# Crossbar transposes for the attention output, and VectorE's part of a first-layer step emitted one step later

## Chip, core and metric

One Trainium2 chip, one of its cores. The metric is the device time of one execution in microseconds; a run of the kernel before and one of the kernel after are compared on the same chip. TensorE is PE, VectorE is DVE, ScalarE is ACT, GpSimd is POOL, SyncE is SP.

## What is computed

Chunked attention over four sequences of 768 positions (8 heads of 64), then a two-layer network on the 3072 resulting rows of 512 numbers:

```python
# per chunk c of 32 positions: keys and values from 16 before to 8 behind it, and 8 memory rows
scores = scale * np.matmul(q_c, k_full.transpose(0, 1, 3, 2))
a = softmax(scores)
out[:, :, c_start:c_end] = np.matmul(a, v_full)
...
x = np.ascontiguousarray(attn_out.transpose(0, 2, 1, 3)).reshape(B * S, H * D)   # 3072 x 512
h = x @ w_in                      # 512 x 2048
s = np.sin(alpha * h)
g = h + s * s / (alpha + 1e-09)
return (g @ w_out).astype(np.float32)   # 2048 x 512
```

## The kernel before

The four sequences (batches) go through one after the other, and the attention of batch i+1 is woven into the second layer of batch i. All matmul operands are bf16, and PE accumulates in PSUM. PSUM is divided into two pools: `big` has three tiles of two banks each (`sc`, `ot`, `hT`, and most of the transposed q and k, `tt_b`), `smp` two tiles of one bank each (`o`, `tt_a`, the split `hs`, `xtp`).

**Attention** (`burst`, L311). A batch has eight blocks of 96 positions. `qk_exp` (L262) computes a block's scores for the eight heads with eight matmuls into `sc` (L266), and ACT takes the exponential into `pt` in three pieces (L275). `pv` (L282) multiplies `pt` with the values, to which a column of ones is added (eight matmuls, L288), and DVE divides by the sum: a reciprocal (L292) and a product (L293) into `x_blk`, 96 positions on partitions by 512 numbers. The first layer needs this with the 512 numbers on partitions. `xt` (L300) makes that: four PE transposes (L306) of 96x128 into PSUM and one DVE copy (L309) into `xT`. For batches 1 to 3 these four go into a part of the bank of `ot` that `pv` has left free; for batch 0 into a tile of `smp`. The burst runs as a software pipeline: in step s the scores of block s, then `pv` of block s-lag, then `xt` of block s-lag-1. Between these three, `stream.take(n)` puts n matmuls of the previous batch's second layer into PE's queue; the numbers are written out by hand in `shares`.

**First layer** (`l1`, L333). A step ft computes 128 of the 2048 hidden columns for all 768 positions: four 128-row slices of the contraction times two halves of 384 positions, eight matmuls (L341) into `hT`, kt outermost. ACT takes the sine into `u` (L353). The square `s2` is taken by ACT, DVE or POOL, as a string of letters says (A, D, P; L356 and L358), and DVE computes gT = s2/alpha + h from PSUM (L367; in two halves, L363, for three steps of batch 0). Only then is the `hT` tile free. Sixteen steps make a batch. In batches 1 to 3, `stream.take(2)` or `take(3)` puts second-layer matmuls of the batch before ahead of each step. In batches 1 and 2 every second step also transposes two heads of the q or k of the batch after the next attention (`piece`): POOL or DVE pairs heads (L226), PE transposes (L242 for k, L257 for q) into the one tile of `smp` that `o` leaves, and DVE copies k (L243, L249) or ACT copies q (L258) to SBUF. Batch 0 does all its eight pieces after its first layer.

**Second layer** (`l2`, L371). Six subtiles of 128 rows per batch, sixteen matmuls of 128x512 each (L393) into `o`, then a copy to `o_sb` by DVE or ACT (L400, L402) and a store by SP (L403). `l2` is a generator; `Stream.take` (L30) advances it. Unless `through` is set, a take stops at the end of a subtile and keeps what is left as a debt for the next take.

**Order.** Each engine runs its instructions in the order in which the program emits them, and waits in place for what an instruction needs; there is no scheduler that moves them. SP's queue holds the output stores; POOL's queue issues the loads of q, k, v and the weights beside POOL's own work. The loads of batch 2 are issued between the pieces and the burst at the end of batch 0, those of batch 3 at the end of batch 1's first layer.

Of the kernel before, what the change touches and what calls it, by code (L numbers as in the profile page):

```python
# [9 lines left out]
P = 128  # L10
QW = 96
NEG = -30000.0
KW = 856
BF = mybir.dt.bfloat16
F32 = mybir.dt.float32
ACTF = mybir.ActivationFunctionType
ALU = mybir.AluOpType
# [28 lines left out]
def kernel(  # L46
# [12 lines left out]
    nc = tc.nc  # L59
    B, H, S, D = q.shape  # L60
# [3 lines left out]
    NJ = S // QW  # L64
    HP = H // 2
    FT = d_ff // P
    KT = d_model // P
    NSUB = S // P
    HALF = S // 2
# [3 lines left out]
    xp = ctx.enter_context(tc.tile_pool(name="xp", bufs=2))  # L73
    gp = ctx.enter_context(tc.tile_pool(name="gp", bufs=2))
    mlp = ctx.enter_context(tc.tile_pool(name="mlp", bufs=3))
    blk = ctx.enter_context(tc.tile_pool(name="blk", bufs=3))
    big = ctx.enter_context(tc.tile_pool(name="big", bufs=3, space=bass.MemoryType.PSUM))
    smp = ctx.enter_context(tc.tile_pool(name="smp", bufs=2, space=bass.MemoryType.PSUM))

# [15 lines left out]
    w_in_sb = consts.tile([P, KT, d_ff], BF, name="w_in_sb")  # L95
    w_out_sb = consts.tile([P, FT, d_model], BF, name="w_out_sb")
    alpha_sb = consts.tile([P, FT], F32, name="alpha_sb")
    inv_alpha = consts.tile([P, FT], F32, name="inv_alpha")
# [13 lines left out]
    def load_qk(b):  # L112
        kb, qb = alloc_qk()
        for src, dst in ((k, kb), (q, qb)):
            nc.gpsimd.dma_start(
                dst[:].rearrange("p h r d -> p h (r d)"),
                src[b].rearrange("h (p r) d -> p h (r d)", p=P),
            )
        return kb, qb
# [47 lines left out]
    def spin(n):  # L167

        z = smp.tile([P, 512], F32, name="z", tag="sm")
        for _ in range(n):  # L170
            nc.tensor.matmul(z[:], zeros[:, 0:P], zeros[:])  # L171
# [19 lines left out]
    for c0, c1, thr, val in (  # L191
# [4 lines left out]
            out=biasm[:, c0:c1], in_=biasm[:, c0:c1],  # L196
# [27 lines left out]
    def pair_up(src, hp, eng=None):  # L224
        pr = blk.tile([P, 6, 2, D], BF, name="pr")
        (eng or nc.gpsimd.tensor_copy)(  # L226
            pr[:].rearrange("p r e d -> p e r d"), src[:, 2 * hp:2 * hp + 2]
        )
        return pr
# [52 lines left out]
    def pv(b, j, pt):  # L282
        x_blk = blk.tile([QW, H, D], BF, name="x_blk")
        rinv = blk.tile([QW, H], F32, name="rinv")
        ot = big.tile([P, 2, 512], F32, name="ot", tag="big")
        otv = ot[:, :, 0:4 * (D + 1)].rearrange("p g (e c) -> p g e c", e=4)
        for h in range(H):
            nc.tensor.matmul(  # L288
                otv[:, h // 4, h % 4, :], pt[:, QW * h:QW * h + P], vws[b % 2][:, h, j, 0:D + 1]
            )  # L290
        rv = rinv[:].rearrange("p (g e) -> p g e", g=2)
        nc.vector.reciprocal(rv, otv[0:QW, :, :, D])  # L292
        nc.vector.tensor_tensor(  # L293
            out=x_blk[:].rearrange("p (g e) d -> p g e d", g=2), in0=otv[0:QW, :, :, 0:D],
            in1=rv.unsqueeze(3).to_broadcast([QW, 2, 4, D]),
            op=ALU.mult,
        )
        return x_blk, ot

    def xt(xT, j, x_blk, ot):  # L300
        if ot is None:
            xtp = smp.tile([P, KT, QW], BF, name="xtp", tag="sm")[:]
        else:
            xtp = ot[:].bitcast(BF)[:, 0, 640:640 + KT * QW].rearrange("p (k c) -> p k c", k=KT)
        for kt in range(KT):
            nc.tensor.transpose(  # L306
                xtp[:, kt, :], x_blk[:, 2 * kt:2 * kt + 2, :].rearrange("p e d -> p (e d)"), ident[0:QW, 0:QW]
            )
        nc.vector.tensor_copy(xT[:, :, QW * j:QW * j + QW], xtp)  # L309

    def burst(b, stream, shares, lag):  # L311

        xT = xp.tile([P, KT, S], BF, name="xT")
        ptl, xbl = {}, {}
        for s in range(NJ + lag + 1):
            n = shares[s] if s < len(shares) else 0
            if s < NJ:
                ptl[s] = qk_exp(s)
            if b == 0:
                spin(1)  # L320
            stream.take(n // 3, True)
            if 0 <= s - lag < NJ:
                xbl[s - lag] = pv(b, s - lag, ptl.pop(s - lag))
                if b == 0:
                    xbl[s - lag] = (xbl[s - lag][0], None)
            stream.take((n + 1) // 3, True)
            if 0 <= s - lag - 1 < NJ:
                xt(xT, s - lag - 1, *xbl.pop(s - lag - 1))
            stream.take((n + 2) // 3, True)
        return xT  # L330


    def l1(i, ft, xT, gT, sq, split=False):  # L333
        if split:
            hts = [smp.tile([P, 512], F32, name="hs", tag="sm") for _ in range(2)]
        else:
            hT = big.tile([P, 2, 512], F32, name="hT", tag="big")
            hts = [hT[:, 0], hT[:, 1]]
        for kt in range(KT):
            for hf in range(2):  # L340
                nc.tensor.matmul(  # L341
                    hts[hf][:, 0:HALF],
                    w_in_sb[:, kt, P * ft:P * ft + P],
                    xT[:, kt, HALF * hf:HALF * hf + HALF],
                    start=(kt == 0), stop=(kt == KT - 1),
                )
        u = mlp.tile([P, 2, HALF], F32, name="u")
        if split:
            for hf in range(2):
                nc.scalar.activation(  # L350
                    u[:, hf], hts[hf][:, 0:HALF], ACTF.Sin, scale=alpha_sb[:, ft:ft + 1])
        else:
            nc.scalar.activation(u[:], hT[:, :, 0:HALF], ACTF.Sin, scale=alpha_sb[:, ft:ft + 1])  # L353
        s2 = mlp.tile([P, 2, HALF], F32, name="s2")
        if sq == "A":
            nc.scalar.activation(s2[:], u[:], ACTF.Square)  # L356
        else:
            (nc.vector if sq == "D" else nc.gpsimd).tensor_tensor(  # L358
                out=s2[:], in0=u[:], in1=u[:], op=ALU.mult)
        gv = gT[:, ft, :].rearrange("p (e c) -> p e c", e=2)  # L360
        for hf in range(2):
            if split:
                nc.vector.scalar_tensor_tensor(  # L363
                    out=gv[:, hf], in0=s2[:, hf], scalar=inv_alpha[:, ft:ft + 1],
                    in1=hts[hf][:, 0:HALF], op0=ALU.mult, op1=ALU.add)
            elif hf == 0:
                nc.vector.scalar_tensor_tensor(  # L367
                    out=gv, in0=s2[:], scalar=inv_alpha[:, ft:ft + 1],
                    in1=hT[:, :, 0:HALF], op0=ALU.mult, op1=ALU.add)

    def l2(i, gT, last=False):  # L371
        for s in range(NSUB):
# [61 lines left out]

    stream = Stream()
    xT = burst(0, stream, (), 2)
    put_memk(1)
    put_memv(1)

    for i in range(B):  # L440
        gT = gp.tile([P, FT, S], BF, name="gT")
        last = i == B - 1
        at_ft = {2 * n: n for n in range(8)}
        pieces = []
        if not last:
            srcs = [(kq_next[n % 2], n // 2) for n in range(2 * HP)]
        state["pools"] = 1

        def pair_to(n):
            while len(pieces) < min(n, 2 * HP):  # L450
                pieces.append(pair_up(*srcs[len(pieces)], nc.vector.tensor_copy if i == 0 and len(pieces) % 2 == 0 else None))

        def piece(n):
            pair_to(n + 3)
            (t_k if n % 2 == 0 else t_q)(pieces[n], n // 2)

        if 0 < i < B - 1:
            pair_to(2)
        for ft in range(FT):
            sq = ("ADADADAAADADADAA" if i == 0 else "ADAAPDADADAPADAD")[ft]  # L460
            if 1 <= ft:
                stream.take(3 if last else 2)
            if 0 < i < B - 1 and ft in at_ft:
                piece(at_ft[ft])
            if i == 0 and ft == 14:
                pair_to(3)
            l1(i, ft, xT, gT, sq, i == 0 and ft in (3, 7, 11))
        stream.add(l2(i, gT, last))
        if not last:
            if i == 0:  # L470
                state["pools"], state["t"] = 3, 0
                stream.take(4)
                for n in range(2 * HP):
                    piece(n)
                    stream.take(3, True)
            if i + 2 < B:
                kq_next = load_qk(i + 2)
            if i == 0:
                xT = burst(i + 1, stream, (3, 3, 3, 4, 4, 4, 4, 4, 4, 4, 5, 5), 3)
            else:  # L480
                xT = burst(i + 1, stream, (16, 8, 6, 6, 6, 5, 5, 5, 5, 5), 1)
            if i + 2 < B:
                put_memk(i + 2)
            stream.take(3)
            if i + 2 < B:
                load_v_all(i + 2)
                put_memv(i + 2)
# [31 lines left out]
```

The softmax here doesn't subtract the row's maximum and nothing guards it: scores larger than these inputs give would overflow.

## Time and profile before

| What | us |
|---|---|
| Runs shown | 243.68, 243.36, 245.46 (median 243.68) |
| The profiled execution's own time | 245.14 |
| Its span, first to last instruction | 243.4 |
| PE busy | 222.6 (91%) |
| DVE busy | 160.2 (66%) |
| ACT busy | 154.7 (64%) |
| POOL busy | 73.3 (30%) |

The page of the profile gives the busy time of each engine, the chain of work that ended last, and the costliest groups of instructions. Some groups that the change touches:

| Group | Count | Busy us | Mean ns |
|---|---|---|---|
| L393 PE, second-layer matmul 128x512 | 368 recorded | 99.0 | 381 |
| L341 PE, first-layer matmul 128x384 | 488 recorded | 88.8 | 329 |
| L306 PE, transposes of x_blk into ot | 96 | 8.1 | 206 |
| L309 DVE, copy of ot to xT | 24 | 8.3 | 344 |
| L367 DVE, gT | 61 | 61.2 | 1012 |
| L358 DVE, square | 24 | 24.7 | 1029 |
| L293 DVE, x_blk | 32 | 22.0 | 686 |
| L243 DVE, copy of k | 16 | 13.6 | 852 and 854 |

A matmul's mean includes the time in which it overlaps its neighbours, since matmuls are pipelined; how closely they follow each other is read from their starts. The stages lie as follows: attention of batch 0 until 29.5 us, its first layer until 54, the pieces and the burst of batch 1 until 80.9, first layer of batch 1 until 112.6, burst of batch 2 until 134.5, first layer of batch 2 until 169.1, burst of batch 3 until 190.9, first layer of batch 3 until 222.5, the rest of its second layer until 243.4.

### The profile page before, as it was taken

To read this page: it belongs to the slowest core of one execution; us is meant where nothing else is said; L and a number is where in the kernel's file an instruction comes from. 1 tells how busy PE (TensorE), PEld (TensorE's weight loads), DVE (VectorE), ACT (ScalarE), POOL (GpSimd) and SP (SyncE) were. 2 spreads that over 40 slices of the span, in tenths; PEclk is the share of its full clock that TensorE was granted. 3 is DMA by queue.
4 is the path that set the end of the run, shared out by engine and by line. 5 is a ranking of instruction groups with operands and counts; after the bars stand their busy time and mean duration, and the time that the engine had idled before them with its cause. 6 is when DMAs were issued, how large, how long until landed. Compare 5 with 4: busy or idle time off the path is not lost.

```text
span 243.4 us, 4498 instructions
## 1 busy us (share of the span) xinstructions
PE 222.6 (91%) x1785; PEld 123.0 (51%) x1785; DVE 160.2 (66%) x287; ACT 154.7 (64%) x237; POOL 73.3 (30%) x96
## 2 busy tenths in 40 slices
PE   6798899989989899898999997998999999899994
PEld 2355565545445455454455653554455555453453
DVE  3496969999268658969457775868657267876101
ACT  3489599973975467798464784678765675871000
POOL 8899865214712114157200222120000002020000
PEclk9799999999999999999999997999999999999999
DMA  6999999999999610109992101001111101101122
GB/s 75 165 130 83 161 194 204 207 198 134 190 208 134 74 46 0 44 4 181 154 151 66 46 0 43 0 3 43 46 43 47 43 0 46 43 0 40 46 89 86
DMA packets 53852, 21.11 MB, mean 87 GB/s; under 512 B 36296, under 2 KB 50888, under 8 KB 53832
## 3 DMA queue, kind: packets, MB, share of 16 engines
q0 software_dynamic: 47616, 14.40, 70.7%
q1 hardware_dynamic: 6216, 6.43, 8.9%
q8 instruction: 14, 0.23, 0.4%
q14 instruction: 6, 0.05, 0.1%
HBM read 28.91 MB, written 6.29 MB: 145 GB/s over the span
## 4 chain that ended last, share of the span: by engine, by line
PE 48%; DVE 20%; ACT 12%; issue 12%; POOL 3%; DMA 2%; POOLq 1%; DVEq 0%; ACTq 0%
PE o L393 26%; PE hT L341 10%; DVE gT L367 8%; DVE s L358 5%; ACT pt L275 4%; ACT u L353 4%; ACT s L356 3%; PE ot L288 3%; PE sc L266 3%; POOL s L358 2%; DMA q_bf<-in_q_dram 2%; DVE kTi L243 2%; PE ot L306 2%; PE o L382 1%; DVE x_blk L293 1%
## 5 line engine op out<-in xcount | busy, mean ns | idle before, releaser
L393 PE MATMUL o<-w_out_sb,gT 128*128 128x512 bf16 x368 | 99.0, 381 | 0.7 <-DVE gT L367 0.4
L341 PE MATMUL hT<-xT,w_in_sb 128*128 128x384 bf16 x488 | 88.8, 329 | 3.9 <-DVE gT L367 3.6
L367 DVE SCALAR_TENSOR_TENSOR gT<-s,inv_alpha,hT 128x768 bf16<-128x768 f32 x61 | 61.2, 1012 | 30.0 <-ACT s L356 21.6
L353 ACT ACTIVATE u<-hT,alpha_sb 128x768 f32<-128x768 f32 x61 | 54.7, 898 | 28.3 <-PE hT L341 27.1
L341 PEld LDWEIGHTS <-w_in_sb 128*128 128x128 bf16 x512 | 49.8, 99 | 39.7 <-issue 7.4
L275 ACT ACTIVATE pt<-sc,biasm 128x256 bf16<-128x256 f32 x96 | 37.6, 492 | 13.0 <-PE sc L266 13.0
L393 PEld LDWEIGHTS <-gT 128*128 128x128 bf16 x368 | 31.9, 98 | 26.9 <-DVE gT L367 1.4
L358 POOL TENSOR_TENSOR s<-u 128x768 f32<-128x768 f32 x6 | 8.8, 1465 | 73.7 <-ACT u L353 73.7
L356 ACT ACTIVATE s<-u 128x768 f32<-128x768 f32 x34 | 28.7, 843 | 1.1
L358 DVE TENSOR_TENSOR s<-u 128x768 f32<-128x768 f32 x24 | 24.7, 1029 | 0.9 <-ACT u L353 0.8
L226 POOL COPY pr<-q_bf 128x768 bf16<-128x768 bf16 x12 | 10.1, 838 | 43.7 <-PE tt_a L242 27.4
L293 DVE TENSOR_TENSOR x_blk<-ot,rinv 96x512 bf16<-96x512 f32 x32 | 22.0, 686 | 1.1
L292 DVE RECIPROCAL rinv<-ot 96x8 f32<-96x8 f32 x32 | 6.4, 201 | 20.1 <-PE ot L288 19.8
L402 ACT COPY o_sb<-o 128x512 f32<-128x512 f32 x11 | 6.4, 585 | 20.0 <-PE o L393 20.0
L400 DVE COPY o_sb<-o 128x512 f32<-128x512 f32 x12 | 8.2, 687 | 15.4 <-PE o L393 15.4
L288 PEld LDWEIGHTS <-pt 128*128 128x128 bf16 x256 | 11.9, 97 | 7.2 <-issue 2.3
L171 PE MATMUL z<-zeros 128*128 128x512 bf16 x37 | 13.9, 463 | 1.3 <-DVE zeros L165 1.3
L288 PE MATMUL ot<-vw,pt 128*128 128x65 bf16 x256 | 13.0, 193 | 0.8 <-ACT pt L275 0.6
L266 PEld LDWEIGHTS <-kTi 64*128 64x128 bf16 x256 | 6.9, 94 | 13.0 <-issue 6.6
L266 PE MATMUL sc<-qT,kTi 64*128 64x96 bf16 x256 | 11.4, 205 | 1.8 <-ACT pt L275 1.2
L257 PEld LDWEIGHTS <-pr 128*128 128x128 bf16 x96 | 6.6, 100 | 12.5 <-issue 8.0
L306 PEld LDWEIGHTS <-x_blk 96*128 96x128 bf16 x128 | 8.4, 97 | 6.6 <-DVE x_blk L293 1.6
(66 smaller groups left out, 182.1 us busy)
## 6 DMA issues: line engine op xcount, KB each, us to landing
out_dram<-o_sb SPq DMA_DIRECT2D x23, 256.0 KB, 2.1
k_bf<-in_k_dram POOLq DMA_DIRECT2D x3, 768.0 KB, 8.6
q_bf<-in_q_dram POOLq DMA_DIRECT2D x3, 768.0 KB, 12.6
vw<-in_v_dram POOLq DMA_DIRECT2D x6, 384.0 KB, 17.4
w_in_sb<-in_moe_w_in_dram POOLq DMA_DIRECT2D x8, 256.0 KB, 8.3
w_out_sb<-in_moe_w_out_dram POOLq DMA_DIRECT2D x4, 512.0 KB, 18.7
k_bf<-in_k_dram POOLq DMA_DIRECT2D x4, 192.0 KB, 6.2
q_bf<-in_q_dram POOLq DMA_DIRECT2D x4, 192.0 KB, 6.7
```

The source lines that it names most:

```text
L171: nc.tensor.matmul(z[:], zeros[:, 0:P], zeros[:])
L266: nc.tensor.matmul(sc[:, e, QW * hp:QW * hp + QW], kTi[64 * e:64 * e + 64, hp, 104 * j:104 * j + P], qT[64 * e:64 * e + 64, hp, QW * j:QW ...
L275: nc.scalar.activation(pt[:, 0:H * QW].rearrange("p (g e c) -> p e g c", g=4, e=2)[:, :, :, 32 * m:32 * m + 32], sc[:, :, 0:4 * QW].rearra ...
L288: nc.tensor.matmul(otv[:, h // 4, h % 4, :], pt[:, QW * h:QW * h + P], vws[b % 2][:, h, j, 0:D + 1])
L293: nc.vector.tensor_tensor(out=x_blk[:].rearrange("p (g e) d -> p g e d", g=2), in0=otv[0:QW, :, :, 0:D], in1=rv.unsqueeze(3).to_broadcast( ...
L306: nc.tensor.transpose(xtp[:, kt, :], x_blk[:, 2 * kt:2 * kt + 2, :].rearrange("p e d -> p (e d)"), ident[0:QW, 0:QW])
L341: nc.tensor.matmul(hts[hf][:, 0:HALF], w_in_sb[:, kt, P * ft:P * ft + P], xT[:, kt, HALF * hf:HALF * hf + HALF], start=(kt == 0), stop=(kt ...
L353: nc.scalar.activation(u[:], hT[:, :, 0:HALF], ACTF.Sin, scale=alpha_sb[:, ft:ft + 1])
L356: nc.scalar.activation(s2[:], u[:], ACTF.Square)
L358: (nc.vector if sq == "D" else nc.gpsimd).tensor_tensor(out=s2[:], in0=u[:], in1=u[:], op=ALU.mult)
L367: nc.vector.scalar_tensor_tensor(out=gv, in0=s2[:], scalar=inv_alpha[:, ft:ft + 1], in1=hT[:, :, 0:HALF], op0=ALU.mult, op1=ALU.add)
L393: nc.tensor.matmul(o[:], gT[:, ft, P * s:P * s + P], w_out_sb[:, ft, :], start=(ft == 0), stop=(ft == FT - 1),)
```

## The change

In batches 1 to 3 the four PE transposes and the DVE copy of a block are replaced by one transposing DMA through the crossbar, from `x_blk` in SBUF to `xT` in SBUF, issued on SP's queue directly after `pv` of the same block. Batch 0 keeps the PE transposes. The pool of `x_blk`, `rinv` and `pr` has four buffers instead of three.

DVE's part of a first-layer step (the square where DVE takes it, and gT) becomes an inner function `finish`, which is called one step later: behind the second-layer matmuls and the piece that are emitted ahead of step ft+1, and before the matmuls of step ft+1. PE's, ACT's and POOL's parts stay in place.

The first step (ft = 0) of a batch runs the four slices of the first half of the positions, then those of the second half.

The hand-written shares of second-layer matmuls in the bursts are lower towards the end, and `stream.take` after a burst takes 8 (batch 0) or 12 instead of 3.

```diff
-    blk = ctx.enter_context(tc.tile_pool(name="blk", bufs=3))
+    blk = ctx.enter_context(tc.tile_pool(name="blk", bufs=4))
...
     def xt(xT, j, x_blk, ot):
-        if ot is None:
-            xtp = smp.tile([P, KT, QW], BF, name="xtp", tag="sm")[:]
-        else:
-            xtp = ot[:].bitcast(BF)[:, 0, 640:640 + KT * QW].rearrange("p (k c) -> p k c", k=KT)
+        if ot is not None:
+            nc.sync.dma_start_transpose(
+                xT[:, :, QW * j:QW * j + QW], x_blk[:].rearrange("p h d -> p (h d)"))
+            return
+        xtp = smp.tile([P, KT, QW], BF, name="xtp", tag="sm")[:]
...
             if 0 <= s - lag < NJ:
-                xbl[s - lag] = pv(b, s - lag, ptl.pop(s - lag))
-                if b == 0:
-                    xbl[s - lag] = (xbl[s - lag][0], None)
+                x_blk, ot = pv(b, s - lag, ptl.pop(s - lag))
+                if b > 0:
+                    xt(xT, s - lag, x_blk, ot)
+                else:
+                    xbl[s - lag] = x_blk
             stream.take((n + 1) // 3, True)
-            if 0 <= s - lag - 1 < NJ:
-                xt(xT, s - lag - 1, *xbl.pop(s - lag - 1))
+            if s - lag - 1 in xbl:
+                xt(xT, s - lag - 1, xbl.pop(s - lag - 1), None)
...
+        order = [(kt, hf) for kt in range(KT) for hf in range(2)]
+        if ft == 0:
+            order.sort(key=lambda o: o[1])
...
+        def finish():
+            if sq == "D":
+                nc.vector.tensor_tensor(out=s2[:], in0=u[:], in1=u[:], op=ALU.mult)
+            gv = gT[:, ft, :].rearrange("p (e c) -> p e c", e=2)
...
+        return finish
...
+        finish = None
         for ft in range(FT):
...
-            l1(i, ft, xT, gT, sq, i == 0 and ft in (3, 7, 11))
+            if finish is not None:
+                finish()
+            finish = l1(i, ft, xT, gT, sq, i == 0 and ft in (3, 7, 11))
+        finish()
...
-                xT = burst(i + 1, stream, (3, 3, 3, 4, 4, 4, 4, 4, 4, 4, 5, 5), 3)
+                xT = burst(i + 1, stream, (3, 3, 3, 4, 4, 4, 4, 4, 4, 4, 5), 3)
             else:
-                xT = burst(i + 1, stream, (16, 8, 6, 6, 6, 5, 5, 5, 5, 5), 1)
+                xT = burst(i + 1, stream, (16, 8, 5, 5, 5, 5, 5, 5, 3), 1)
...
-            stream.take(3)
+            stream.take(8 if i == 0 else 12)
```

More of the change, by code (lines that the diff above doesn't have):

```diff
@@ L338, in l1 @@
             hts = [hT[:, 0], hT[:, 1]]
[L339 to L346, printed above, removed]
+        order = [(kt, hf) for kt in range(KT) for hf in range(2)]
+        if ft == 0:
+            order.sort(key=lambda o: o[1])
+        for kt, hf in order:
+            nc.tensor.matmul(
+                hts[hf][:, 0:HALF],
+                w_in_sb[:, kt, P * ft:P * ft + P],
+                xT[:, kt, HALF * hf:HALF * hf + HALF],
+                start=(kt == 0), stop=(kt == KT - 1),
+            )
         u = mlp.tile([P, 2, HALF], F32, name="u")
@@ L356, in l1 @@
             nc.scalar.activation(s2[:], u[:], ACTF.Square)
[L357 to L369, printed above, removed]
+        elif sq == "P":
+            nc.gpsimd.tensor_tensor(out=s2[:], in0=u[:], in1=u[:], op=ALU.mult)
+        def finish():
+            if sq == "D":
+                nc.vector.tensor_tensor(out=s2[:], in0=u[:], in1=u[:], op=ALU.mult)
+            gv = gT[:, ft, :].rearrange("p (e c) -> p e c", e=2)
+            for hf in range(2):
+                if split:
+                    nc.vector.scalar_tensor_tensor(
+                        out=gv[:, hf], in0=s2[:, hf], scalar=inv_alpha[:, ft:ft + 1],
+                        in1=hts[hf][:, 0:HALF], op0=ALU.mult, op1=ALU.add)
+                elif hf == 0:
+                    nc.vector.scalar_tensor_tensor(
+                        out=gv, in0=s2[:], scalar=inv_alpha[:, ft:ft + 1],
+                        in1=hT[:, :, 0:HALF], op0=ALU.mult, op1=ALU.add)
+        return finish
     def l2(i, gT, last=False):
```

## The prediction

> **What bounds the kernel now.** I read first the table by stretches, with the cuts put where the batches' stages change, then the waits of TensorE, then the groups by form, then the timeline at the end of an attention burst, and last the DMA view of two stretches. Columns of the first fence: stretch, length, then busy time (and instructions) of PE, PE weight load, DVE, ACT and POOL, granted clock, DMA share, GB/s.
>
> ```profile
> 29.50:54.00 24.50, 22.96 (x140) 13.27 (x140) 21.74 (x28) 21.90 (x29) 10.11 (x11) 1.00 1.32 201
> 80.90:112.60 31.70, 27.82 (x190) 16.49 (x190) 24.10 (x34) 23.79 (x29) 12.10 (x12) 1.00 0.19 37
> 112.60:134.50 21.90, 21.90 (x237) 11.53 (x237) 14.19 (x31) 13.38 (x29) 3.39 (x5) 1.00 1.77 134
> 134.50:169.10 34.60, 31.30 (x205) 17.76 (x204) 24.70 (x33) 23.31 (x29) 7.12 (x7) 0.95 0.06 22
> 169.10:190.90 21.80, 21.76 (x231) 11.15 (x228) 13.51 (x29) 14.09 (x30) 0.00 (x0) 1.00 0.10 38
> ```
>
> The bursts of batches 2 and 3 (lines 3 and 5) are TensorE without a gap: work taken off PE there comes off the time. The first-layer stages of batches 1 and 2 (lines 2 and 4) leave PE idle for 3.9 and 3.3 us. Batch 0 (line 1) is bound by the DVE and ACT chain. Who stops PE:
>
> ```profile
> PE hT L341 <- DVE gT L367: 3.6, 6, 1.1
> ...
> PE tt_a L257 <- DVE o_sb L400: 3.1, 2, 1.7
> ...
> PE tt_a L257 <- DVE kTi L249: 2.4, 3, 1.0
> ```
>
> Total, times, longest. The last two are the transposes of q that wait for a PSUM tile which DVE has yet to empty; DVE is late because it stands in a previous step's gT. After the longest of them (1.73 us, until 147.72) the clock falls:
>
> ```profile
> 147.00:148.00 1.00, 0.28 (x5) 0.27 (x5) 1.00 (x3) 0.00 (x0) 0.00 (x0) 1.00 0.00 0
> 149.00:150.00 1.00, 1.00 (x5) 0.46 (x4) 0.66 (x1) 0.06 (x1) 0.22 (x1) 0.50 0.24 88
> ```
>
> The four stretches from 148 to 152 read 0.68, 0.50, 0.50 and 0.62: 0.32+0.50+0.50+0.38 = 1.7 us of PE work lost. A wait of 1.35 us (before 85.69) had no such drop.
>
> The end of the last burst, where the xT of the next first layer is completed:
>
> ```profile
> 187.57 0.41 PE L288 MATMUL ot<-vw,pt 128*128 128x65 bf16 x8
> 187.82 0.59 PE L393 MATMUL o<-w_out_sb,gT 128*128 128x512 bf16 x2
> 188.01 0.20 DVE L292 RECIPROCAL rinv<-ot 96x8 f32<-96x8 f32 x1 [0.31 <-PE ot L288]
> 188.25 0.33 PE L306 MATMUL ot<-ident,x_blk 96*128 96x96 bf16 x4
> 188.25 0.69 DVE L293 TENSOR_TENSOR x_blk<-ot,rinv 96x512 bf16<-96x512 f32 x1
> 188.42 1.24 PE L393 MATMUL o<-w_out_sb,gT 128*128 128x512 bf16 x5
> ...
> 190.75 1.46 PE L341 MATMUL hT<-xT,w_in_sb 128*128 128x384 bf16 x8
> ```
>
> From starts, since PE ends overlap: four transposes cost 188.42-188.25 = 0.17 us of PE; an L393 matmul 0.2155 us (five from 189.67, then 190.75); a first-layer step 1.30 us (8 x 0.163, from the chain of waits). The last x_blk is ready at 188.94, which is 1.12 us after PE is done with L288 (187.82).
>
> **The Trainium skill.** "VectorE: DVE Perf Modes", section "The three transpose paths", gives 1309 ns for a 128x128 bf16 crossbar transpose and 390 ns for TensorE's. No trace here has the first; the second is not borne out in this pipeline, where a 96x128 one costs PE 0.17/4 = 0.04 us. "Advanced Engine Details and Errata", section "X-Bar Transpose (TRN2)", says that transposing DMAs are as fast as ordinary ones; no run here shows it. "DMA: Bandwidth & Descriptors", section "Issuing engines are not separate DMA queues", says that DMAs of all queues interleave on the same 16 engines. The trace agrees: the same 256 KB output store lands in 2.0 us late in the kernel and in 5.5 us between 60 and 85 us, where the loads of batch 2 run:
>
> ```profile
> out_dram<-o_sb SPq DMA_DIRECT2D x13, 256.0 KB, 2.0
> ...
> out_dram<-o_sb SPq DMA_DIRECT2D x3, 256.0 KB, 5.5
> ```
>
> **The change, part by part.** *TensorE's transposes go* in batches 1 to 3: 3 x 8 x 0.17 = 4.1 us, all on the bound. The 24 DVE copies (L309, 0.344 us each, 8.3 us) go too; DVE has slack in the bursts (13.5 of 21.8 us), so they count nothing.
>
> *The deferral.* In every step DVE now meets the o_sb copy and the kTi copies of step ft+1 before the square and gT of step ft. ACT needs 0.90+0.84 us for sine and square before gT can run anyway, and the copies (0.85+0.31, or 0.69) mostly fit into that. The o_sb waits should go whole (3.1 us), of the kTi waits I count half (1.2), since the last steps of batch 1 are DVE-bound and only move the wait: 4.3 us, bounds 2 and 5.5. The clock drop went with the 1.73 us wait: 1.7 more. POOL's squares and ACT's part stay where they are. What can be late instead is hT: a gT behind both kTi copies comes up to 1.2 us later, and step ft+3 waits for that hT (three PSUM pairs). I count 0, since three steps take over 4 us of PE; bound +1.5.
>
> *The first step's order.* In batch 0 the first half no longer waits for the last xT copy; half of 1.30 us lies earlier: 0.6 us.
>
> *Gains:* 4.1+4.3+1.7+0.6 = 10.7 us.
>
> *What the crossbar adds.* On SP's queue, behind output stores, 24 DMAs of 96 KB; each waits for x_blk, so a store behind it waits too (o_sb has three buffers and a store comes every 4 us: free). x_blk has four buffers, so DVE stops if one takes longer than four blocks. And xT is now complete only when the last DMA lands. The PE order after the last L288 of a burst is 12, 9 and 9 second-layer matmuls (the take stops at a subtile's end), six key transposes (0.33 us) in batches 1 and 2, then the four first-half matmuls (0.65 us). Cover from x_blk to need, less the 1.12 us: batch 1 2.59+0.33+0.65-1.12 = 2.45; batch 2 1.94+0.33+0.65-1.12 = 1.80; batch 3 1.94+0.65-1.12 = 1.47 us. Issue to landing of one crossbar transpose isn't in the trace. From below: 1.7 us, the 128 KB store. From above: four times the skill's 1309 ns, 5.2 us. I take 3.0 us on free engines and 5.5 under load (the store's). Batch 1's burst lies wholly under the loads (they end at 81.5), batch 2's last blocks don't (129). Waits: 5.5-2.45 = 3.0; 3.0-1.80 = 1.2; 3.0-1.47 = 1.5; sum 5.7. The wait of 3.0 is longer than the one that dropped the clock: +1.7. The takes only move second-layer matmuls, 96 per batch as before: 0. More pr buffers: 0, no PE wait is on pr after batch 0.
>
> *Sum:* 10.7 gained, 7.4 given back: -3.3 us. The profiled execution took 245.14 us with a span of 243.4; it should become about 241.8 and 240.1. The median of the three runs shown is 243.68, 1.5 below the profiled one, so **240.4 us**.
>
> **Rivals.** *Crossbar hidden.* Landing in about 2.0 us, load or not: waits 0+0.2+0.5, no clock drop: -10, 233.7; with the deferral at its low bound and the +1.5, 237.5; I say 235.5. For it: 96 KB is less than a store. Against: stores go to 5.5 under load.
>
> *Slower: the crossbar queue falls behind.* Eight blocks must pass between the first x_blk and the need: in batch 1 66.99 to about 80.0 = 13 us, batch 2 118.5 to 133.8 = 15.3. That is 1.6 to 1.9 us per block. If a block occupies the queue longer than that, waits add up over eight. If each 1 KB row of x_blk went in four pieces (a guess), that is 384 packets, 24 per DMA engine; at the mean 56 ns of a packet on SP's queue (8.9% of 16 engines' 243.4 us over 6216 packets) 1.3 us, and beside loads, sharing the engines with them, twice that: 2.6. Then batch 1 waits 8x2.6+1-13 = 8.8, batch 2 about 5 (the loads end at 129), batch 3 1.5, and two clock drops 3.4: 18.7-10.7 = +8, 251.7; with part of the blocks after the loads, 249. It decides from about 2.1 us per block. For it: the DMA share of 1.8 to 2.5 in those bursts. At 5.2 us per block, eight take 42 us, some 28 more than there is, three times: above 300 us.
>
> *The deferral does nothing* because the waits move to hT: -10.7+6.0+7.4 = +2.7 at worst; with less waiting for xT 244.5.
>
> **How the numbers follow.** Within 1% is what a measurement of this kernel can't tell from no change: 241.2 to 246.1. Forecast 0.40 (238.5 to 243: 0.26 faster, 0.14 same), hidden 0.18 (faster), queue behind 0.30 (0.03 same, 0.27 slower), one block at 5.2 us 0.06 (slower), deferral idle 0.06 (0.05 same, 0.01 slower). Faster 0.44, same 0.22, slower 0.34. Range 235 to 252 leaves out the 5.2 us case, the upper part of the queue case and a little below. The forecast's own range is 238.5 to 243.
>
> **What would show it.** No L306 in bursts after the first, PE 1.36 us shorter in each; no waits tt_a on o_sb; a wait of L346 for xT from a DMA at its fifth matmul in each of batches 1 to 3, 3.0, 1.2 and 1.5 us. Wrong if that wait is near zero three times, if it grows beyond 5 us, if x_blk waits for a DMA, or if hT's waits for gT pass 5 us.

## The result, and the profile after

The kernel after takes **254.52 us** (median, 254.2 to 257.29) against 243.85 us for the kernel before on the same chip: ratio 1.045, 95% interval 1.036 to 1.054. The forecast was 240.4. The profiled execution has a span of 252.5 us (before 243.4) and a mean granted clock of 0.959 (before 0.986).

The stages are cut at the first scores (`sc`) of a batch's attention and at the first sine (`u`) of its first layer, so that waiting for `xT` falls into the attention burst (us):

| Kernel | burst 1 | 1st layer, batch 1 | burst 2 | 1st layer, batch 2 | burst 3 | rest |
|---|---|---|---|---|---|---|
| before | 20.51 | 30.34 | 23.42 | 32.98 | 23.29 | 51.15 |
| after | 30.16 | 29.06 | 26.16 | 31.18 | 22.09 | 52.44 |
| difference | +9.65 | -1.28 | +2.74 | -1.80 | -1.20 | +1.29 |

With -0.30 ahead of burst 1 these add up to the 9.1 us between the spans. The loss is made in bursts 1 and 2; the other stages gain, apart from the last, which takes over six second-layer matmuls (6 x 0.2155 = 1.3 us) that the lower shares push out of burst 3. The same 1.3 us moves from burst 2 into the first layer of batch 2.

From the page of the kernel after: the granted clock in 40 slices, the chain that ended last by engine, and two groups (busy us, mean ns, then idle time before them and what ended most of it).

```profile
PEclk9899999999999559999999979999999999999999
...
PE 50%; DMA 14%; DVE 13%; issue 9%; POOL 8%; ACT 5%; POOLq 1%; SPq 0%; DVEq 0%; ACTq 0%
...
L346 PE MATMUL hT<-xT,w_in_sb 128*128 128x384 bf16 x488 | 90.2, 333 | 18.3 <-DMA xT<-x_blk 14.9
...
L293 DVE TENSOR_TENSOR x_blk<-ot,rinv 96x512 bf16<-96x512 f32 x32 | 22.0, 687 | 13.9 <-DMA xT<-x_blk 13.1
```

Two engines wait for the same DMA, for different reasons. PE waits because `xT` isn't complete; DVE waits because all four `x_blk` buffers are held by transposes that haven't landed. The waits of the kernel after, all engines (total us, times, longest):

```profile
PE hT L346 <- DMA xT<-x_blk: 14.9, 5, 7.3
...
DVE x_blk L293 <- DMA xT<-x_blk: 13.1, 8, 2.9
...
PE hT L346 <- DVE gT L375: 3.4, 6, 1.1
```

`tt_a` no longer waits for `o_sb` or kTi with any weight, as the deferral intended. The end of burst 1 shows how the two waits follow each other (start, length, engine and line; in brackets the idle time before it and what ended it):

```profile
74.75 0.69 DVE L293 TENSOR_TENSOR x_blk<-ot,rinv 96x512 bf16<-96x512 f32 x1 [2.13 <-DMA xT<-x_blk]
...
81.57 0.69 DVE L293 TENSOR_TENSOR x_blk<-ot,rinv 96x512 bf16<-96x512 f32 x1 [2.68 <-DMA xT<-x_blk]
...
81.61 1.21 PE L346 MATMUL hT<-xT,w_in_sb 128*128 128x384 bf16 x4 [2.77 <-DMA xT<-x_blk]
...
82.28 1.39 SPq L302 DMA_TRANSPOSE xT<-x_blk  x1
...
90.10 1.44 PE L346 MATMUL hT<-xT,w_in_sb 128*128 128x384 bf16 x4 [7.28 <-DMA xT<-x_blk]
```

The eighth block can be written only at 81.57, when an earlier transpose has landed and freed a buffer; its own transpose is issued at 82.28 and lands at 90.05, and PE stands still for 7.28 us. Already the first half of the positions had cost 2.77. In burst 2 the same pair is 0.78 and 2.53, in burst 3 only 1.50 for the second half.

How long a transpose takes from its issue until its data has landed depends on what else the DMA engines do. From the DMA view of the kernel after, in the stretches 66 to 83, 125 to 146 and 183 to 199 us (issues, KB each where shown, median us to landing):

```profile
out_dram<-o_sb SPq DMA_DIRECT2D x3, 256.0 KB, 5.6
xT<-x_blk SPq DMA_TRANSPOSE x8, 9.6
...
xT<-x_blk SPq DMA_TRANSPOSE x8, 7.9
...
xT<-x_blk SPq DMA_TRANSPOSE x8, 2.9
```

These medians rest on few records: the trace has the landing of three, five and two of the eight transposes, and of one store of the three. The chain of waits adds 9.17 and 7.77 us for two more in burst 1 and 10.14 for one in burst 2. Burst 2 shows both conditions within one burst: the three recorded while v was being loaded took 7.9 to 9.5 us, and the two issued at 142.18 and 143.50, when the last load of v landed (142.59), took 2.3.

The last thing to read is the clock behind the waits (stretch, length, busy us and instructions of PE, PE weight load, DVE, ACT and POOL, granted clock, DMA share, GB/s):

```profile
92.00:94.00 2.00, 2.00 (x7) 0.88 (x6) 1.31 (x2) 1.32 (x2) 0.00 (x0) 0.50 0.00 0
94.00:96.00 2.00, 2.00 (x12) 1.01 (x11) 0.48 (x2) 0.90 (x1) 0.00 (x0) 0.62 0.35 131
...
148.00:150.00 2.00, 2.00 (x6) 0.76 (x5) 1.01 (x1) 0.57 (x1) 0.00 (x0) 0.50 0.00 0
...
81.88:95.53 13.65, 6.14 (x19) 2.56 (x18) 4.52 (x8) 2.29 (x3) 0.00 (x0) 0.50 1.00 94
146.74:150.15 3.41, 3.41 (x11) 1.29 (x9) 1.01 (x1) 1.74 (x2) 0.00 (x0) 0.50 0.00 0
```

The last two lines have the edges at which the clock changed. In batch 1 it fell at 81.88, just behind the first wait (2.77 us, until 81.61), and was still at half when the second ended, so PE works at half clock from 90.1 to about 95.5. With 0.4 us lost at 81.6 to 82.8, that is 0.4 + 0.9 + 1.0 + 0.8 = 3.1 us of PE work; behind batch 2's waits (146.74 to 150.15) it is half of 3.41, 1.7.

### The profile page after: what moved, and what is told of

Its sections match the earlier page's. It is cut to its first block, busy times and chain, and to the rows that moved or that the text cites. A ratio compares the mean times of both kernels' runs of the same rounds, so it can differ in the third digit from the quotient of the medians.

```text
span 252.5 us, 4325 instructions
## 1 busy us (share of the span) xinstructions
PE 219.4 (87%) x1665; PEld 120.4 (48%) x1689; DVE 152.2 (60%) x263; ACT 154.1 (61%) x237; POOL 73.0 (29%) x96
## 3 DMA queue, kind: packets, MB, share of 16 engines
q1 hardware_dynamic: 16200, 8.79, 17.3%
## 4 chain that ended last, share of the span: by engine, by line
PE 50%; DMA 14%; DVE 13%; issue 9%; POOL 8%; ACT 5%; POOLq 1%; SPq 0%; DVEq 0%; ACTq 0%
PE o L403 24%; PE hT L346 17%; DMA xT<-x_blk 13%; DVE gT L375 6%; DVE x_blk L293 3%; ACT u L358 3%; DVE s L367 3%; PE sc L266 2%; POOL vw L129 2%; PE ot L288 2%; POOL vw L125 2%; ACT s L361 2%; PE o L392 1%; POOL s L363 1%; POOL q_bf L102 1%
## 5 line engine op out<-in xcount | busy, mean ns | idle before, releaser
L346 PE MATMUL hT<-xT,w_in_sb 128*128 128x384 bf16 x488 | 90.2, 333 | 18.3 <-DMA xT<-x_blk 14.9
L403 PE MATMUL o<-w_out_sb,gT 128*128 128x512 bf16 x345 | 91.7, 386 | 2.5 <-issue 0.7
L403 PEld LDWEIGHTS <-gT 128*128 128x128 bf16 x368 | 33.8, 99 | 33.7 <-issue 2.6
L293 DVE TENSOR_TENSOR x_blk<-ot,rinv 96x512 bf16<-96x512 f32 x32 | 22.0, 687 | 13.9 <-DMA xT<-x_blk 13.1
L367 DVE TENSOR_TENSOR s<-u 128x768 f32<-128x768 f32 x24 | 23.9, 995 | 5.6 <-ACT u L358 5.5
L288 PEld LDWEIGHTS <-pt 128*128 128x128 bf16 x256 | 11.7, 98 | 8.0 <-issue 2.9
L288 PE MATMUL ot<-vw,pt 128*128 128x65 bf16 x256 | 13.0, 193 | 2.8 <-DVE x_blk L293 2.1
L226 POOL COPY pr<-k_bf 128x768 bf16<-128x768 bf16 x8 | 6.6, 826 | 18.5 <-PE tt_a L242 11.9
## 6 DMA issues: line engine op xcount, KB each, us to landing
vw<-in_v_dram POOLq DMA_DIRECT2D x6, 384.0 KB, 22.8
```

The source lines that it names most:

```text
L226: (eng or nc.gpsimd.tensor_copy)(pr[:].rearrange("p r e d -> p e r d"), src[:, 2 * hp:2 * hp + 2])
L288: nc.tensor.matmul(otv[:, h // 4, h % 4, :], pt[:, QW * h:QW * h + P], vws[b % 2][:, h, j, 0:D + 1])
L293: nc.vector.tensor_tensor(out=x_blk[:].rearrange("p (g e) d -> p g e d", g=2), in0=otv[0:QW, :, :, 0:D], in1=rv.unsqueeze(3).to_broadcast( ...
L346: nc.tensor.matmul(hts[hf][:, 0:HALF], w_in_sb[:, kt, P * ft:P * ft + P], xT[:, kt, HALF * hf:HALF * hf + HALF], start=(kt == 0), stop=(kt ...
L367: nc.vector.tensor_tensor(out=s2[:], in0=u[:], in1=u[:], op=ALU.mult)
L403: nc.tensor.matmul(o[:], gT[:, ft, P * s:P * s + P], w_out_sb[:, ft, :], start=(ft == 0), stop=(ft == FT - 1),)
```

## Experiments

All ratios are to the kernel before, run on the same chip. Its median was between 243.85 and 244.67 us there, so a difference of less than a microsecond between kernels run on different chips says little. Everything else alone, eight buffers and the copy in 96 pieces have two executions each.

### The two halves of the change

*Deferral alone* is the kernel before with `finish` called one step later:

```diff
+            if finish is not None:
+                finish()
+            finish = l1(i, ft, xT, gT, sq, i == 0 and ft in (3, 7, 11))
+        finish()
```

> The kernel before with the deferral of VectorE's part alone (PE transposes, shares and order of halves as before). Theory 'crossbar': all of the loss comes from the crossbar, and the deferral by itself gains what the waits tt_a on o_sb and on kTi were worth: 238.4 us (237.5 to 240). Rival 'deferral': gT later, so hT is freed later and the first layers lose: 245 or more.

*Everything else alone* is the kernel after with the deferral undone:

```diff
-            if finish is not None:
-                finish()
-            finish = l1(i, ft, xT, gT, sq, i == 0 and ft in (3, 7, 11))
-        finish()
+            l1(i, ft, xT, gT, sq, i == 0 and ft in (3, 7, 11))()
```

> The kernel after without the deferral. Theory 'crossbar': the loss gets larger by what the deferral gains, about 258 us (256 to 260), with the waits tt_a on o_sb back. Rival 'deferral': 250 or less.

Deferral alone: 236.53 us, 0.969 (0.963 to 0.976). The rest alone: 256.27 us, 1.049 (1.040 to 1.059), with 15.5 us of PE waits for `xT`, the longest again 7.3. So the deferral is a gain and all of the loss is in the rest. The gain isn't the clock's alone: the kernel before has a median of 243.77 us in the 20 executions (of 48) that kept a clock of 0.998 or more, 7.2 more than the deferral alone. The longest PE waits of the deferral alone:

```profile
PE hT L341 <- DVE gT L370: 3.5, 6, 1.3
...
PE ot L288 <- ACT o_sb L407: 1.1, 1, 1.1
```

The waits of `tt_a` for `o_sb` and kTi (3.1 and 2.4 us before) have gone from the list, hT waits for gT no more than before (3.6), and the clock is 1.0 throughout. Its first layers take 27.02 and 28.00 us, against 30.34 and 32.98.

The two halves don't add: deferral is worth 8.1 us alone but 1.75 (256.27 to 254.52) beside the rest. Part of that is plain: without deferral but with the rest, `tt_a` waits only 0.9 us for `o_sb` and 1.3 for kTi, so little is left for it to remove, and of the 5.0 us in batch 2's first layer 1.7 were a clock drop that the wait for `xT` now brings anyway. (The intervals of these two kernels overlap; in the stages the deferral is worth 0.97 and 0.98 us in the two first layers beside the rest.) PE starts both first layers late and at half clock, which leaves DVE time. That this is why DVE keeps up is an inference; no run isolates it.

*The takes alone*: the kernel before with the shares and takes of the kernel after.

```diff
-                xT = burst(i + 1, stream, (16, 8, 6, 6, 6, 5, 5, 5, 5, 5), 1)
+                xT = burst(i + 1, stream, (16, 8, 5, 5, 5, 5, 5, 5, 3), 1)
...
-            stream.take(3)
+            stream.take(8 if i == 0 else 12)
```

> The kernel before with the changed shares and takes alone (PE transposes, no deferral). The deferral alone gained 8 us, but only 1.8 us in the presence of the crossbar. Theory 'moved subtile ends': the changed takes move the o_sb copies to other steps, so the waits of tt_a on o_sb (3.1 us) and the clock drop behind them go without the deferral: 239 to 241.5. Rival: the takes do nothing by themselves, and the deferral's gain was eaten by the clock drops after the waits for xT: 243 to 245.5.

244.28 us, 0.999 (0.996 to 1.003): no difference. In its profile one of the two `tt_a` waits for `o_sb` was gone (1.4 us left) and batch 2's first layer was down to 30.74 at clock 1.0. The median didn't gain by it: three of its other executions had a clock of 0.986, as the profile of the kernel before has, so this one profile doesn't show that the takes spare the clock drop.

*Deferral and the order of halves, no crossbar*:

```diff
-XBAR = (3,)
+XBAR = ()
```

(`XBAR` lists the batches that use the crossbar; the others keep PE transposes, shares and takes of the kernel before.)

> Deferral and the order of the first step's halves, with PE transposes, shares and takes of before: no crossbar at all. Theory: the order gains what the first batch's first step showed, 0.3 to 0.6 us over the deferral alone, 236.0; so the crossbar in batch 3 (235.8) was worth nothing. Rival: the order does nothing, 236.5, and the crossbar without loads gained 0.7 us.

237.17 us, 0.968 (0.964 to 0.973), with stages equal to those of deferral alone within 0.03 us from burst 1 on. The order of halves gains nothing that shows in the whole time. Its gain is in the traces: from the end of batch 0's last `x_blk` to the first sine it takes 2.18 us in the kernel before and 2.19 with the deferral alone, and 1.74 with the order of halves, here and in the kernel after. These 0.44 us drown in the scatter ahead of burst 1 (61.33 us in the profile of the deferral alone, 62.19 here, with a half clock from 8.05 to 14.88).

### The crossbar where there are no loads

*Crossbar in batch 3 only*, the rest of the change kept (`XBAR = (3,)`):

> The kernel after with the crossbar in batch 3 alone, where no loads run; batches 1 and 2 have PE transposes, shares and takes of before. Theory 'loads': the loss needs the loads beside the transposes, so this is as fast as the deferral alone or a little faster, 238 us (237 to 239.5), with a wait for xT of about 1.5 us in batch 3. Rival 'SP issue': each transpose holds SP's queue for 1.2 us wherever it stands, a third of the loss of 9 to 16 us stays, 241 to 244.

*The same with cover* (PE work between the last `x_blk` and the matmul that needs it): behind the last block of batch 3 a whole subtile of second-layer matmuls is put in PE's queue.

```diff
-            stream.take((8 if i == 0 else 12) if i + 1 in XBAR else 3)
+            if i + 1 in XBAR:
+                stream.take(16, True)
+            else:
+                stream.take(3)
```

> The crossbar in batch 3 alone, with 16 second-layer matmuls behind the last block instead of the 9 at which the take stops. Theory: the wait for xT (1.1 us in batch 3) goes and the 1.36 us that PE no longer spends on transposes show: 234.9 (234.3 to 235.4). Rival: what is moved behind the last block is missing later, 235.8.

235.79 us, 0.966 (0.959 to 0.972), and 235.22 us, 0.964 (0.960 to 0.967). The transposes land in 2.3 us (median) in both. PE waits 1.1 us for `xT` in the first and not at all in the second. This is the fastest version run. Against 237.17 without any crossbar it is 1.95 us less by the medians, but the intervals of the two ratios overlap. The stages say what the crossbar is worth in batch 3: burst 3 and all behind it take 74.20 us without it, 73.98 with it and 72.96 with it and cover, a gain of 1.24 us, near the 1.36 of the transposes. Of the 2.10 us between the two profiled spans the other 0.87 lie ahead of burst 1, where neither kernel uses the crossbar.

### Loads, buffers, or the queue

The theory: the transposes are late because they share the DMA engines with the loads of the next values (v), which run through bursts 1 and 2. The rival: the ring of four `x_blk` buffers is what stops DVE and delays the last transposes.

*Eight buffers* in the kernel after:

```diff
+    xbp = ctx.enter_context(tc.tile_pool(name="xbp", bufs=8))
...
-        x_blk = blk.tile([QW, H, D], BF, name="x_blk")
+        x_blk = xbp.tile([QW, H, D], BF, name="x_blk")
```

> The kernel after with eight x_blk buffers of their own instead of four. Rival 'ring': the four buffers hold VectorE back (13 us of waits for the DMA), the last block is issued some 5 us sooner in batch 1, and the time falls to about 248 to 250 us. Theory 'loads': VectorE no longer waits, but the last transpose still lands when the loads end, at about 89 us in batch 1; 252.5 to 255 us.

*v later*: the loads of v for batches 2 and 3, and the copy of the memory rows behind them, move from after the previous burst into the first layer that follows it.

```diff
+            if i in (1, 2) and ft == 5:
+                load_v_all(i + 1)
+                put_memv(i + 1)
...
-            if i + 2 < B:
-                load_v_all(i + 2)
-                put_memv(i + 2)
```

> The kernel after with the loads of v for batches 2 and 3 (and the copy of the memory values into them) issued inside the next first layer, at its sixth step, instead of beside the attention burst; q and k stay where they are. Theory 'loads': in the bursts of batches 1 and 2 the transposes then land in 2 to 4 us once q and k are in, the waits of TensorE for xT fall from 14.9 us to about 4, the clock drops behind them go, and the time is about 239 us (237 to 242). Rival 'crossbar itself': eight transposes in a row are slow on SP's queue with or without loads, and the time stays above 248 us.

*Both*:

> The same with eight x_blk buffers of their own. Theory 'loads': without the v loads the four buffers are enough, so no change against the late v loads alone (within 1 us). Rival 'ring': another 2 to 3 us less, as with the loads in place.

| Kernel | us | Ratio (95%) | PE waits for `xT` | Landing, median |
|---|---|---|---|---|
| after | 254.52 | 1.045 (1.036-1.054) | 14.9 | 8.1 |
| eight buffers | 251.87 | 1.031 (1.022-1.041) | 14.5 | 8.6 |
| v later | 242.07 | 0.990 (0.984-0.996) | 4.8 | 2.3 |
| both | 239.18 | 0.978 (0.971-0.985) | 4.5 | 2.8 |

The landing is a median over the 10 landings (of 24) that each trace has, all three bursts together. Moving the loads takes off 12.4 us, eight buffers 2.6. The loads are the main cause. The ring is likely a second, smaller one: DVE's waits for buffers go, and burst 1 is 28.05 us instead of 30.16, but the intervals with and without eight buffers overlap. With v later the profile keeps no half clock (two other executions had 0.986), and the waits for the transposes read:

```profile
PE hT L346 <- DMA xT<-x_blk: 4.8, 3, 2.8
DVE x_blk L293 <- DMA xT<-x_blk: 3.0, 2, 2.4
```

The difference of 2.9 us between "v later" and "both", which the rival "ring" had expected, isn't clean: in the profiled execution of "v later" PE also waited 2.6 us in burst 1 for batch 1's own values, which "both" did not, and nothing in the edit asks for that.

With eight buffers DVE never waits for a transpose, but something else comes next. Its end of burst 1, from two timelines of that kernel (SP's queue, then PE):

```profile
76.11 2.45 SPq L303 DMA_TRANSPOSE xT<-x_blk  x1
...
79.28 1.23 SPq L303 DMA_TRANSPOSE xT<-x_blk  x1
80.57 0.81 PE L347 MATMUL hT<-xT,w_in_sb 128*128 128x384 bf16 x4 [2.66 <-DMA xT<-x_blk]
87.48 1.44 PE L347 MATMUL hT<-xT,w_in_sb 128*128 128x384 bf16 x4 [6.11 <-DMA xT<-x_blk]
```

The eighth `x_blk` was ready at 75.95, but its transpose was issued at 79.28: SP was busy with the seventh for 2.45 us and then with a store for 0.53. Each transpose occupies SP's queue for 1.2 us or more, while the last blocks come every 1.11 us (73.04, 74.15, 75.26 for their products). So blocks that are ready sooner queue on SP, and the landing beside the loads is as long as before.

*v later, crossbar in batches 2 and 3 only*:

> Late v loads, deferral, crossbar in batches 2 and 3, PE transposes in batch 1. Candidate for the fastest: with the crossbar in batch 3 alone it was 235.8; batch 2 should add a gain like batch 3's if the v loads were the cause: 235 (234 to 236.5). If q and k alone still hold the transposes up in batch 2: 237 to 239.

237.97 us, 0.975 (0.968 to 0.983): not better than leaving v where it was with the crossbar in batch 3 alone. Each first layer is 0.75 us or more longer (27.76 and 30.87 against 27.02 and 28.01; the second has the 1.3 us of moved matmuls too), since hT now waits 5.8 us for gT where it waited about 3.5. DVE's copy of the memory rows runs there, and the square that POOL computes beside it is longer:

```profile
90.20 1.22 DVE L154 COPY vw<-memv_st 8x4096 bf16<-8x4096 bf16 x1
90.21 2.53 POOL L367 TENSOR_TENSOR s<-u 128x768 f32<-128x768 f32 x1 [8.96 <-DVE gT L379]
```

In the three kernels with v later this happens twice each, and the square takes 2.53 or 2.54 us all six times instead of 1.46 to 1.47, so gT, which needs it, comes later. The copy's own 1.22 us lie mostly in time in which DVE would have waited for that square anyway (1.55 and 0.94 us in batches 1 and 2 without the copy). Moving the loads has a price of its own.

### The crossbar, or any DMA at that place

Two kernels put a plain SBUF-to-SBUF copy where the transpose is, everything else as in the kernel after. Both leave the transposition out: the numbers go to `xT` untransposed, three quarters of them (72 KB), and the rest of `xT` is zero. The first copies 384 pieces of 192 bytes, the second 96 pieces of 768.

```diff
-            nc.sync.dma_start_transpose(
-                xT[:, :, QW * j:QW * j + QW], x_blk[:].rearrange("p h d -> p (h d)"))
+            nc.sync.dma_start(
+                xT[0:QW, :, QW * j:QW * j + QW],
+                x_blk[:].rearrange("p (k e) d -> p k (e d)", e=2)[:, :, 0:QW])
...
+        if b > 0:
+            nc.vector.memset(xT[QW:P], 0.0)
```

> The kernel after with each crossbar transpose replaced by an ordinary SBUF to SBUF copy in as many pieces (384 of 192 bytes; the transpose is left out, so xT holds untransposed data and zeros on 32 partitions). Theory 'shared engines': what counts is the pieces that wait their turn beside the loads' packets; landing in batches 1 and 2 stays near 8 us and the time near 252 us. Rival 'crossbar itself': an ordinary copy lands in 3 to 4 us there and the time falls below 245 us.

```diff
+            nc.sync.dma_start(
+                xT[0:QW].rearrange("p k s -> p (k s)")[:, 384 * j:384 * j + 384],
+                x_blk[:].rearrange("p h d -> p (h d)")[:, 0:384])
```

> The same with 96 pieces of 768 bytes (the transpose is left out here too, and the data of a block lies in one run of xT). Theory 'shared engines, by pieces': a quarter of the pieces waits less; landing about 4 to 5.5 us as the output stores' in the same stretch, time 240 to 246 us. Rival 'by bytes or by the fixed wait for the loads' packets': as with 384 pieces.

384 pieces: 245.16 us, 1.004 (1.001 to 1.006), PE waits for `xT` 8.6 us, DVE for buffers 10.1. 96 pieces: 241.38 us, 0.988 (0.982 to 0.995), waits 5.9 and 8.1. Landing of the first, in the stretches 64 to 81, 121 to 140 and 178 to 196 us:

```profile
xT<-x_blk SPq DMA_DIRECT2D x7, 72.0 KB, 7.6
...
xT<-x_blk SPq DMA_DIRECT2D x8, 72.0 KB, 7.5
...
xT<-x_blk SPq DMA_DIRECT2D x8, 72.0 KB, 2.6
```

A plain copy is late beside the loads too, with few pieces as with many (7.5 us median in both bursts for the second), and with free engines it lands about when a transpose does. In landing the transposes add little to that: recorded beside the loads are 7.9 to 9.6 us for transposes, 7.2 to 9.0 and 7.2 to 8.7 for the copies, which move three quarters of the bytes. On SP's queue they take twice the time. The tile view of the copy and of the transpose (min/median/max ns on the queue):

```profile
L302 SPq DMA_DIRECT2D xT<-x_blk x24: 589/592/992, 67.5 to 188.7; - x24
```

```profile
L302 SPq DMA_TRANSPOSE xT<-x_blk x24: 1181/1222/2046, 67.0 to 196.7; - x24
```

Measured from 237.17 us (deferral and order without crossbar), the kernel after loses 17.4 us, the copy in 384 pieces 8.0, the copy in 96 pieces 4.2, and the crossbar with v later 4.9. So neither loads nor crossbar alone gives the loss: a quarter (96 pieces) to almost half of it (384) comes with a plain copy that is waited for beside those loads, the rest with the transposing DMA. Both expectations for 384 pieces failed in part, since the landing stayed near 8 us and the time fell to 245: how long one DMA takes to land isn't what sets these kernels apart.

What does go with the time is when the loads end. The loads of v for batch 2 are issued from 60.1 to 64.7 us in every kernel; the traces have, in burst 1 (us):

| Kernel | Last load of v landed | PE went on after its last wait for `xT` |
|---|---|---|
| before | 82.24 | no such wait |
| copy, 96 pieces | 84.77 | 84.64 |
| copy, 384 pieces | 87.22 | 87.53 |
| after, eight buffers | 88.51 | 87.48 |
| everything else alone | 90.09 | 89.79 |
| after | 90.63 | 90.10 |

In all five kernels PE goes on within 1.1 us of the end of the loads, whenever the last block was issued (79.3 to 82.7), and the loads themselves end 2.5 to 8.4 us later than without these DMAs. That fits transfers and loads that hold each other up. Which property of a transpose prolongs the loads most (its packets, its bytes or its time on the queue) no run isolates.

## Why the prediction was wrong

**PE's transposes, 4.1 us: right as far as it shows.** In bursts 1 and 2 the waits cover it. Burst 3 shows it without loads: 23.29 - 1.36 (transposes) - 1.3 (matmuls moved out) + 1.50 (wait) = 22.13; measured 22.09.

**The deferral, 4.3 plus 1.7 for the clock: right in its mechanism, too small in its term.** Alone it gives 8.1 us, and in the first layers 3.3 + 5.0 = 8.3, of which 1.7 is the clock. The waits went, kTi's whole and not by half: 3.1 + 2.4 = 5.5 of the 6.6 us that are left without the clock. For the other 1.1 no wait was named. Beside the late transposes only 1.75 remain.

**First step's order, 0.6: 0.44** at that step, and not seen in the whole time (236.53 without it, 237.17 with it, the intervals overlap). **Takes, 0: right**, 0.999.

**The wait for `xT`, 5.7 us: here the forecast failed.** The step that failed was "5.5 under load (the store's)", 3.0 for batch 2 because its "last blocks don't" lie under the loads, and a sum of cover against one landing, with the loads ending where they had ended before (81.5 and 129). Burst 3, the one with free engines, has the number: 1.5 predicted, 1.50 measured. That is in part luck. The eighth transpose landed 2.33 us after its issue, and 0.67 us had gone between its `x_blk` (196.08) and its issue (196.75), behind the seventh on SP's queue: the 3.0 us came from two parts, of which the prediction had one. Bursts 1 and 2 gave 2.77 + 7.28 = 10.05 for 3.0 and 0.78 + 2.53 = 3.31 for 1.2. Three things were missing:

- *The landing.* The store's 5.5 us was taken as the price of the loads for any DMA. It was the landing of one store, issued at 66.08, the only one of the three that the trace records. After the change such a store takes 5.6, the transposes behind it 8.4 to 9.6, and in burst 2 one issued at 132.39 took 10.14 by the chain of waits. The loads' end before the change couldn't be used as theirs after it: with the transposes, the 384 KB loads of v land in 22.8 us (median), before in 17.4, and the last load of v ends at 90.63 instead of 82.24 in burst 1 and at 142.59 in burst 2, just when PE's first wait there ends (142.59). The wait in burst 1 lasts as long as the loads.
- *The ring*, dismissed with "DVE stops if one takes longer than four blocks" and no number. Four buffers and a landing of 9.6 us allow one block per 2.4 us, and burst 1 has 1.6. Eight buffers win 2.6 us back, with intervals that overlap.
- *SP's queue.* The prediction asked what a store loses behind a transpose, not what a transpose loses behind other transposes: 1.22 us each. What this costs by itself isn't shown: with eight buffers the eighth was issued 3.3 us after its `x_blk` was ready, but PE went on only 1.0 us before the loads ended.

**The clock, 1.7 us: 4.8.** Two drops, 3.1 behind batch 1's waits and 1.7 behind batch 2's. The 1.7 us gained for the drop of before was counted twice: it is read from the profiled execution, which had that drop, while the 1.5 us by which the median lies below that execution was taken off as well. Of the 48 executions of the kernel before that were taken with the experiments, 20 had a clock of 0.998 or more and a median of 243.77 us, and 15 had 0.985 or 0.986 and 245.19. So those 1.5 us are mostly that drop, and 240.4 should have been about 242.

With the measured terms the sum between the two profiled executions closes: -4.1 for the transposes, -6.6 for the deferral's waits (8.3 less 1.7), -1.7 for the clock drop of before, +14.9 waits for `xT`, +2.1 that PE waited for `x_blk` in L288, +4.8 for the two new clock drops and -0.3 ahead of burst 1 make +9.1, the difference of the spans. The term of -6.6 is carried over from the run of the deferral alone; the stages agree with it (batch 1's first layer: 30.34 - 3.3 + 2.0 of half clock behind its first `u` = 29.04, measured 29.06).

**The slower rival, at 0.30, is what happened**, "the crossbar queue falls behind": it had 8.8 us for batch 1, about 5 for batch 2, 1.5 for batch 3 and two clock drops of 3.4, for 10.05, 3.31, 1.50 and 4.8. It guessed 384 packets for a transpose; the 24 added 16200 - 6216 = 9984 packets to SP's queue, 416 each (the copies in 384 and 96 pieces 400 and 112). What it had wrong is the place: 2.6 us of engine time per block, where it was landing over ring (2.4), SP's issue (1.2 to 2.4) and loads that end later. That its totals come so near is therefore in part luck. The prediction put no measurement against it; its own forecast rested on the 5.5 us of a store, a DMA of another kind.

**What was named as a sign of being wrong came true twice**: the wait grew beyond 5 us (7.28), and `x_blk` waited for a DMA (13.1). The Trainium skill, "Advanced Engine Details and Errata", section "X-Bar Transpose (TRN2)", says that transposing DMAs are as fast as ordinary ones. For landing on free engines the runs agree (medians of 2.3 to 2.9 us against 2.6), beside loads nearly (7.9 to 9.6 against 7.2 to 9.0 for fewer bytes); on the issuing queue and in the time of the kernel they don't (1222 ns against 592, 254.52 us against 245.16), and there the measurement decides.

## What to carry to other kernels

When work moves from an engine to a DMA that something waits for, price the DMA in the stage where it runs, with the loads of that stage, and by a DMA of its own kind if there is any; then ask four questions in a row: when does it land, when do the loads end once it runs beside them, how many may be in flight before a buffer stops the producer, and how long does one occupy the queue that issues it. A part of a change that gains (here the deferral, 3.1%) can be hidden whole by one that loses, so run the parts singly, and keep the losing one where its conditions hold (here only batch 3, where nothing is loaded). Small parts are read from the stages of the traces (0.44 us for the order, 1.24 for the crossbar in batch 3), since the whole time scatters by as much or more.

## What was not expected of the hardware

- A small DMA from SP, transposing or not, 72 or 96 KB, took 7.2 to 9.8 us to land beside the loads of v in the kernels with four buffers, and 1.9 to 4.5 us in the last burst, where no load ran; 96 pieces instead of 384 changed the medians beside the loads by 0.1 us. The loads in turn ended up to 8.4 us later.
- One transpose occupied SP's queue for 1.18 to 2.45 us, twice or more the 0.59 (median) of a plain copy in 384 pieces.
- The clock didn't follow the length of a single wait: in the profiled executions it fell within 1 us behind waits of 2.77 and 2.53 us after the change and behind 1.73 before, but not behind 2.83 with v later, nor behind 1.50 in burst 3. It also differs between executions of one kernel (1.0 in some, 0.986 in others). Where it fell behind a wait, it stayed at half for 3.41 us or a multiple of it: 3.42 before, 13.65 and 3.41 after, 10.24 and 6.8 with eight buffers. What decides when it falls stays open.
- A square on POOL took 2.53 us instead of 1.47 when DVE's copy of the memory rows started at the same time.
